# A gated mixer on one core: the last 128 columns of w2 computed turned for three chunks of four, and w3's load placed earlier in SyncE's queue

## The chip, the cores and the metric

One core of a Trainium2 chip runs the kernel. Its time is the device time of one execution in microseconds (us). Where a time is read from the profile, it is the time from the start of the profiled span.

## What is computed

Input x has 2048 rows (tokens) of D = 640 columns, bf16. The output is g·a + (1−g)·b, where g is a sigmoid of a dot product per row, a is a linear attention with 32 heads of 20 columns, and b is a mixer:

```
h  = gelu(layernorm(x) @ w1)                 # w1: 640 x 640
hs = shift(h) @ w2                           # four column groups shifted by 1, -1, 2, -2 rows; w2: 640 x 640
x1 = x + hs
b  = x1 + gelu(layernorm(x1) @ w3) @ w4      # w3: 640 x 1728, w4: 1728 x 640
a  = (phi(q) @ kv) / (phi(q) . z) @ wo       # kv and z: sums over all rows
```

The change touches `x1 = x + hs` and when w3 is loaded.

## The kernel before, in words

The rows are 16 tiles of 128 (numbered t or u), and 4 chunks of 512 (numbered c). TensorE (PE) multiplies; a matmul is at most 128x128 stationary against 512 moving columns, and a product over 640 takes five. ScalarE (ACT) applies gelu and squares, VectorE (DVE) adds into `x_tok` and normalises q, GpSimd (POOL) does the small layernorm statistics and the normalisation, and SyncE (SP) issues most DMAs, in one queue in program order. Among them are crossbar transposes ("turns", L281), which turn 128-wide blocks from SBUF to SBUF.

The stages that matter here, with short names for the steps:

- **w1(c,j)**, c = 0..3, j = 0..4 (`w1_group`, L1109): five matmuls of 512 columns, and gelu into `hsT` on ACT, shifted by rows. The fifth group (j = 4) holds parts of all four shifts, and its gelu is four ACT instructions of 32 partitions.
- **t0..t15** (`w2_tile`, L1117): for one tile, five times a 512-column matmul (L624) and a 128-column one that keeps the same stationary block (L613). DVE then adds the 640 columns of PSUM into `x_tok` and leaves the row sums (L662). The last tile of a chunk also needs rows of the next chunk: t3, t7 and t11 wait for the gelu of w1(c+1, 4).
- **sq t** (`w2_sq`, L1123): ACT squares x_tok's 640 columns and leaves the sum of squares (L680).
- **s2 c** (`ln_chunk_stats`, L859): seven small POOL instructions per chunk, after the chunk's four squares.
- **n2 u** and **T2 u** (L884, L890): POOL normalises tile u into one of three `xn` buffers; SP turns it into `xnT`. The buffer is free again when the turn has landed.
- **w3(c,j)**, j = 0..12 (`w3_group`, L1126): five matmuls of 512 columns and one gelu (`h2T`). w3(c,0) needs T2 of all four tiles of its chunk.
- **M0, M1** (`m_last`, `m_first`, L1066, L1071): the small products that make the matrix `M_sb` of the attention; ACT and DVE copy it out. **mt** (L1080): five small DMAs on SP then put rows into `M_sb`.
- **q-turn t** (L1178): SP turns the normalised q of tile t into `pqnT`.
- **a0..a15** (`a_tile`, L1229): five matmuls with `M_sb` that open the output tiles. a0 needs q-turn 0 and all five DMAs of mt.
- Then w4, the output and the end.

The order of the instructions is written neither by hand nor at run time. `_Items.run` (L336) holds each step as an item of a stream with dependencies and, at build time, always takes the item that can start first by the planner's own costs. PSUM's eight banks are given out by `bank()` (L519): the one that the planner thinks is free first. So an item that becomes later moves others, on every engine, and may make a matmul wait for another bank. Within an engine, instructions run in the planned order. x_tok is bf16; `mw` and `mtok` (L509, L510) lie in memory that the attention's `pk_tok` used earlier.

In the kernel before, w3's and w4's loads stand together on SP behind the turn of q's fourth chunk (L1377, L1378): w3 first, 2160 KB, then w4 in three DMAs, 2080 KB and twice 80 KB.

The w4 stage already computes its last 128 columns turned: `w4_turned` (L1294) multiplies with the weight block as stationary operand and 512 rows as moving columns, copies the result with ACT into `mw`, and turns it back with one DMA into `mtok`.

Of the kernel before, what the change touches and what calls it, by code (L numbers as in the profile page):

```python
# [7 lines left out]
ACTF = mybir.ActivationFunctionType  # L8
ALU = mybir.AluOpType

S = 2048
D = 640
# [3 lines left out]
NT = S // 128  # L16
NCH = S // 512
KD = D // 128
# [398 lines left out]
def _build(nc, A_x, A_wqkv, A_wo, B_w1, B_w2, B_w3, B_w4, gate_w, out, dbg=None, stop=None):  # L417
    sch = _Sched(nc)
# [41 lines left out]
    ps = nc.alloc_psum_tensor("ps", [128, 8, 512], F32)  # L460
# [10 lines left out]
    st2 = pa.alloc("st2", [128, 8, NT], F32)  # L471
# [4 lines left out]
    w2 = pa.alloc("w2", [128, KD, D], BF16)  # L476
    wo_aug = pa.alloc("wo_aug", [128, 6, D], BF16)
    x_tok = pa.alloc("x_tok", [128, NT, D], BF16)
    xnT = pa.alloc("xnT", [128, KD, S], BF16)
    hsT = pa.alloc("hsT", [128, KD, S + 4], BF16)  # L480
# [28 lines left out]
    mw = rb.alloc("mw", [128, 2, 512], BF16)  # L509
    mtok = rb.alloc("mtok", [128, 2, 4, 128], BF16)  # L510
# [8 lines left out]
    def bank():  # L519
        best = None  # L520
        for k_ in range(nbanks[0]):
            b = (bank_rr[0] + k_) % nbanks[0]
            if b in bank_pend or b in bank_hold:
                continue
            lk = sch.locks.get(b)
            tfree = 0.0 if lk is None else sch.ev_time.get((lk[1].sem, lk[1].val), 1e18)
            if best is None or tfree < best[0]:
                best = (tfree, b)
        bank_rr[0] = best[1] + 1
        bank_pend.add(best[1])  # L530
        return best[1]
# [30 lines left out]
    def nfree(ap):  # L562
        n = 1
        for d_ in ap.shape[1:]:
            n *= d_
        return n

    def in_psum(ap):
        return ap.tensor.name == ps.name

    def act(fn, reads, writes, cost=None):
        if cost is None:
            n = nfree(writes[0])
            cost = max(150.0, 100.0 + 0.833 * n + (70.0 if (reads and in_psum(reads[0])) else 0.0))
            cost += 45.0 * max(0, len(reads) - 1)
        return sch.op("act", fn, reads, writes, cost=cost)

    def dve(fn, reads, writes, cost=None):
        if cost is None:
            n = nfree(writes[0])  # L580
            cost = 65.0 + n / 0.96
        return sch.op("dve", fn, reads, writes, cost=cost)
# [7 lines left out]
    def pe(fn, reads, writes, cost=500.0, after=None):  # L590
        for w_ in writes:
            sp_, rl = sch.rects(w_)
            if sp_ == "ps":
                for (_p0, _p1, lo, hi) in rl:
                    for b in range(lo // PS_BANK, (hi - 1) // PS_BANK + 1):
                        bank_pend.discard(b)
        return sch.op("pe", fn, reads, writes, cost=cost, after=after)

    def mm_group(out_ap, pairs, reads_extra=()):
        n = len(pairs)  # L600

        def fn(e, out_ap=out_ap, pairs=pairs, n=n):
            ins = None
            for i, (l, r) in enumerate(pairs):
                ins = e.matmul(out_ap, l, r, start=(i == 0), stop=(i == n - 1))  # L605
            return ins
        reads = [a for p in pairs for a in p] + list(reads_extra)
        return pe(fn, reads, [out_ap], cost=n * (max(nfree(pairs[0][1]), 24) * 0.4167 + 2.5))
# [40 lines left out]
    def tt(engf, out_ap, a, b_, op):  # L649
        cost = None  # L650
        if engf is pool:
            cost = 1000.0 if op == ALU.pow else 200.0 + 2.3 * nfree(out_ap)
        elif not in_psum(a):
            cost = 830.0
        return engf(lambda e: e.tensor_tensor(out_ap, a, b_, op), [a, b_], [out_ap], cost=cost)  # L655

    def stt(out_ap, in0, scalar, in1, op0, op1, accum=None):
        rd = [in0, in1] + ([scalar] if not isinstance(scalar, (int, float)) else [])
        n = nfree(out_ap)
        cost = (65.0 + n / 0.96) if (in_psum(in0) or in_psum(in1)) else (160.0 + 1.04 * n)  # L660
        if accum is not None:
            return dve(lambda e: e.scalar_tensor_tensor(out_ap, in0, scalar, in1, op0, op1, accum_out=accum), rd,  # L662
                       [out_ap, accum], cost=cost + 70.0)
        return dve(lambda e: e.scalar_tensor_tensor(out_ap, in0, scalar, in1, op0, op1), rd, [out_ap], cost=cost)  # L664
# [3 lines left out]
    def activation(out_ap, in_ap, func, scale=1.0, bias=0.0, accum=None):  # L668
        rd = [in_ap] + [a for a in (scale, bias) if not isinstance(a, (int, float))]
        wr = [out_ap] + ([accum] if accum is not None else [])  # L670
        n = nfree(out_ap)
        cost = max(150.0, 100.0 + 0.833 * n + (70.0 if in_psum(in_ap) else 0.0)) + 45.0 * (len(rd) - 1)
        if accum is not None:
            cost += 91.0
        st_ = ACT_SET.get(func)
        if st_ is not None and st_ != sch.act_func:
            cost += 1290.0
            sch.act_func = st_
        if accum is not None:
            return act(lambda e: e.activation(out_ap, in_ap, func, bias=bias, scale=scale, accum_out=accum), rd, wr, cost=cost)  # L680
        return act(lambda e: e.activation(out_ap, in_ap, func, bias=bias, scale=scale), rd, wr, cost=cost)  # L681
# [105 lines left out]
    def tag_set(buf, sl, what):  # L787
        tags[(buf, sl)] = what

    def tag_chk(buf, sl, what):  # L790
        assert tags.get((buf, sl)) == what, ("stale ring slot", buf, sl, what, tags.get((buf, sl)))

    IT = _Items()
# [65 lines left out]
    def ln_chunk_stats(st, c, rs):  # L859
        cs = slice(4 * c, 4 * c + 4)  # L860
        ts(pool, st[:, 2, cs], rs, 1.0 / D, 0.0, ALU.mult, ALU.add)
        ts(pool, st[:, 3, cs], st[:, 1, cs], 1.0 / D, EPS_LN, ALU.mult, ALU.add)
        tt(pool, st[:, 4, cs], st[:, 2, cs], st[:, 2, cs], ALU.mult)
        tt(pool, st[:, 5, cs], st[:, 3, cs], st[:, 4, cs], ALU.subtract)
        tt(pool, st[:, 6, cs], st[:, 5, cs], negh[:, 0:4], ALU.pow)
        tt(pool, st[:, 7, cs], st[:, 2, cs], st[:, 6, cs], ALU.mult)
        ts(pool, st[:, 7, cs], st[:, 7, cs], -1.0, 0.0, ALU.mult, ALU.add)
# [101 lines left out]
    for i in range(3, NT + 2):  # L969
        if i < NT:  # L970
            addA(("q", i), 1.08, lambda t=i: q_tile(t))
            addA(("k", i), 1.36, lambda t=i: k_tile(t))
            if i % 4 == 3:
                addA(("qx", i // 4), 1.08, lambda c=i // 4: q_turned(c))
                IT.add("QB", ("qb", i // 4), 0.0, lambda c=i // 4: q_back(c),
                       deps=[(("qx", i // 4), 2.5), (("t1", NT - 1), 0.0) if i == NT - 1 else (("k", i + 1), 0.0)])
# [140 lines left out]
    def w2_tile(t):  # L1117
        tok = slice(2 + 128 * t, 2 + 128 * (t + 1))
        b = pair()
        mm_both((ps[:, b, 0:512], ps[:, b + 1, 0:128]), [(hsT[:, k, tok], w2[:, k, 0:512], w2[:, k, 512:D]) for k in range(KD)])  # L1120
        stt(x_tok[:, t, :], psf[:, 512 * b:512 * b + D], 1.0, x_tok[:, t, :], ALU.mult, ALU.add, accum=st2[:, 0, t:t + 1])

    def w2_sq(t):  # L1123
        activation(junk[:, 0, :], x_tok[:, t, :], ACTF.Square, accum=st2[:, 1, t:t + 1])

# [222 lines left out]
    for c in range(NCH):  # L1348
        for j in range(KD):
            deps = [(("t1", u), 0.9) for u in range(4 * c, 4 * c + 4)] if j == 0 else []  # L1350
# [7 lines left out]
    for t in range(NT):  # L1358
        c = t // 4
        deps = [(("w1", c, KD - 1), GEL)]  # L1360
        if t % 4 == 3 and c + 1 < NCH:
            deps.append((("w1", c + 1, KD - 1), GEL))
        if t == 0:
            deps.append((("g", KD - 1), 0.0))
        IT.add("W2", ("w2", t), 1.33, lambda t=t: w2_tile(t), deps)
        IT.add("SQ", ("sq", t), 0.0, lambda t=t: w2_sq(t), [(("w2", t), 1.0)])
        if t % 4 == 3:
            IT.add("S2", ("s2", c), 0.0, lambda c=c: ln_chunk_stats(st2, c, st2[:, 0, 4 * c:4 * c + 4]), [(("sq", t), 1.0)])
    for u in range(NT):
        deps = [(("s2", u // 4), 3.2 + 0.9 * (u % 4))]  # L1370
        if u >= 3:
# [2 lines left out]
            deps.append((("t1", NT - 3 + u), 0.0))  # L1374
        IT.add("N2", ("n2", u), 0.0, lambda u=u: normalize(2, u, st2), deps)
        IT.add("T2", ("t2", u), 0.0, lambda u=u: t_xn(2, u), deps=[(("n2", u), 1.1)] + ([(("mt",), 0.0)] if u == 12 else []))
    IT.add("MISC", ("w3load",), 0.0, w3_load, deps=[(("qb", NCH - 1), 0.0), (("k", NT - 1), 0.0), (("t1", NT - 1), 0.0)])  # L1377
    IT.add("MISC", ("w4load",), 0.0, w4_load, deps=[(("qb", NCH - 1), 0.0), (("kvt", 1), 0.0), (("t1", NT - 1), 0.0), (("z", NT - 1), 1.5)])  # L1378
    for c in range(NCH):
        for j in range(KFF):  # L1380
            deps = []
# [4 lines left out]
            if j == 0:  # L1386
                deps = deps0 + [(("t2", u), 0.9) for u in range(4 * c, 4 * c + 4)]
# [12 lines left out]
    for t in range(NT):  # L1400
        deps = [(("zb",), 1.0), (("q", max(t, 2)), 2.0), (("sg", 1), 0.0)]
# [13 lines left out]
    for t in range(NT):  # L1415
        g = GOF[t]
        t0, t1 = GROUPS[g]
        cl = (t1 - 1) // 4
        deps = [(("qt", t), 3.0), (("w4load",), 0.0), (("m", 1), 1.0), (("mt",), 2.5)]
# [66 lines left out]
```

## Time and profile before

| | |
|---|---|
| median of 3 runs | 259.38 us (258.87 to 259.90) |
| the profiled execution's own time | 258.86 us |
| its span | 257.6 us (1.26 us lie outside) |
| PE busy | 254.5 us, 99% of the span |
| DVE, ACT, POOL busy | 143.1, 108.5, 89.8 us |
| granted TensorE clock | 1.0 |

The span is the time from the first to the last instruction of the profiled execution. A matmul's record overlaps the next one's, so a matmul's pace is read from the distance of starts and not from its duration. The chain of work that ended last goes back from the last instruction, at each step to whatever released it. A group's line gives line number, engine, operation, out<-in tiles, shapes and count, then busy time and mean ns of one, then the idle time before them and what ended it. In the timeline, the columns are start, length, engine, line, operation, tiles and shapes; merged rows say how many instructions they hold.

### The profile page before, as it was taken

How to read it: one execution, taken by the hardware profiler on the slowest of the kernel's cores; microseconds unless marked ns; L12 is line 12 of the kernel's file. 1: busy time of each engine (PE TensorE's matmuls, PEld its weight loads, DVE VectorE, ACT ScalarE, POOL GpSimd, SP SyncE). 2: the span in 40 equal slices, each digit the busy share in tenths (PEclk: the TensorE clock that was granted, in tenths of full speed). 3: DMA queues.
4: the chain of work that ended last, by engine and by line, in shares of the span. 5: the costliest groups of instructions: out<-in, count | busy, mean ns of one | idle time of the engine just before them, and what ended most of it. 6: DMA issues, size and time to landing. Idle time of an engine off the chain costs nothing.

```text
span 257.6 us, 3610 instructions
## 1 busy us (share of the span) xinstructions
PE 254.5 (99%) x1418; PEld 110.5 (43%) x1242; DVE 143.1 (56%) x289; ACT 108.5 (42%) x222; POOL 89.8 (35%) x146
## 2 busy tenths in 40 slices
PE   8999999999999999999999999999999999999997
PEld 4333333344454333334444444444444444444444
DVE  2687888899953995489999400689300033200033
ACT  1586676651356867665854230003520100253000
POOL 5020499966762153667905200423000021300000
DMA  7878699946843699552536631022200112200012
GB/s 221 232 160 199 133 132 163 241 90 127 116 92 77 97 343 356 107 103 51 115 24 127 127 79 20 0 82 73 51 0 0 23 24 99 102 1 3 0 20 102
DMA packets 57825, 26.48 MB, mean 103 GB/s; under 512 B 49188, under 2 KB 56397, under 8 KB 57808
## 3 DMA queue, kind: packets, MB, share of 16 engines
q1 hardware_dynamic: 54976, 21.87, 38.8%
q0 software_dynamic: 1168, 3.28, 6.1%
q10 hardware_dynamic: 1664, 1.11, 1.4%
q8 instruction: 10, 0.16, 0.3%
q14 instruction: 7, 0.06, 0.1%
HBM read 12.04 MB, written 2.62 MB: 57 GB/s over the span
## 4 chain that ended last, share of the span: by engine, by line
PE 96%; DMA 2%; SPq 1%; issue 0%; DVE 0%
PE ps L605 37%; PE ps L1239 30%; PE ps L624 14%; PE ps L830 7%; PE ps L613 4%; DMA wkg<-in_A_wqkv_dram 2%; SPq L285 1%; PE ps L1285 1%; PE ps L1146 1%; PE ps L941 1%; PE ps L1028 0%; PE ps L1057 0%; DVE x_tok L664 0%
## 5 line engine op out<-in xcount | busy, mean ns | idle before, releaser
L605 PE MATMUL ps<-xnT,w 128*128 128x512 bf16 x360 | 81.3, 379 | 0.0
L664 DVE SCALAR_TENSOR_TENSOR x_tok<-ps,stg,abx 128x512 bf16<-128x512 f32 (+2 forms) x17 | 12.2, 719 | 81.9 <-PE ps L1239 81.8
L681 ACT ACTIVATE h2T<-ps 128x512 bf16<-128x512 f32 x52 | 30.6, 598 | 59.3 <-PE ps L605 59.3
L605 PEld LDWEIGHTS ps<-xnT,w 128*128 128x128 bf16 x360 | 34.5, 98 | 41.6 <-issue 2.4
L1239 PE MATMUL ps<-w,h2T 128*128 128x512 bf16 (+2 forms) x221 | 45.4, 366 | 0.0
L647 POOL TENSOR_SCALAR xn<-x_tok,st 128x640 bf16<-128x640 bf16 x32 | 34.4, 1082 | 29.2 <-DMA xnT<-xn 28.7
L647 POOL TENSOR_SCALAR abx<-x_tok,stg 128x640 f32<-128x640 bf16 (+1 forms) x16 | 15.0, 945 | 69.3 <-DVE x_tok L664 69.3
L1239 PEld LDWEIGHTS ps<-w,h2T 128*128 128x128 bf16 x221 | 21.2, 98 | 24.1
L681 ACT ACTIVATE Er<-ps 128x512 bf16<-128x512 f32 (+1 forms) x36 | 23.0, 648 | 14.6 <-PE ps L613 11.0
L680 ACT ACTIVATE junk<-x_tok 128x640 bf16<-128x640 bf16 x32 | 23.6, 738 | 3.9 <-DVE x_tok L662 3.7
L681 ACT ACTIVATE hsT<-ps 128x512 bf16<-128x512 f32 (+1 forms) x32 | 19.0, 594 | 12.5 <-PE ps L605 12.0
L624 PE MATMUL ps<-w,hsT 128*128 128x512 bf16 x80 | 23.0, 379 | 0.0
L624 PE MATMUL ps<-wkg,xT 128*128 128x512 bf16 x70 | 20.7, 379 | 0.0
L662 DVE SCALAR_TENSOR_TENSOR x_tok<-ps,x_tok 128x640 bf16<-128x640 f32 x16 | 13.1, 822 | 11.0 <-PE ps L613 10.5
L1239 PE MATMUL ps<-M_sb,pqnT 128*128 128x512 bf16 (+2 forms) x85 | 18.6, 367 | 0.0
L830 PE MATMUL ps<-pk_tok,x_tok 128*128 128x512 bf16 x80 | 17.8, 379 | 0.0
L1175 DVE TENSOR_TENSOR pq_tok<-pq_tok,dnr 128x300 bf16<-128x300 bf16 (+1 forms) x48 | 17.4, 416 | 0.5
L613 PE MATMUL ps<-wkg,xT 128*128 128x130 bf16 x80 | 17.6, 219 | 0.0
L613 PE MATMUL ps<-w,hsT 128*128 128x128 bf16 x80 | 17.5, 219 | 0.0
L647 DVE TENSOR_SCALAR Er<-Er 128x512 bf16<-128x512 bf16 (+1 forms) x36 | 12.2, 339 | 7.4 <-ACT Er L681 6.7
L605 PE MATMUL ps<-wq,xT 128*128 128x512 bf16 x65 | 16.1, 379 | 0.0
L655 DVE TENSOR_TENSOR qprod<-qprod,pk_tok 128x640 f32<-128x640 f32 x13 | 15.2, 1166 | 0.5
(90 smaller groups left out, 250.4 us busy)
## 6 DMA issues: line engine op xcount, KB each, us to landing
w<-in_B_w_dram SPq DMA_DIRECT2D x1, 2160.0 KB, 8.4
w<-in_B_w_dram SPq DMA_DIRECT2D x1, 2080.0 KB, 14.1
out_dram<-x_tok SPq DMA_DIRECT2D x3, 640.0 KB, 3.2
w<-in_B_w_dram POOLq DMA_DIRECT2D x8, 160.0 KB, 5.8
x_tok<-in_A_x_dram SPq DMA_DIRECT2D x6, 160.0 KB, 3.7
x_tok<-in_A_x_dram SPq DMA_DIRECT2D x1, 960.0 KB, 5.8
wv<-in_A_wqkv_dram POOLq DMA_DIRECT2D x1, 800.0 KB, 5.7
x_tok<-in_A_x_dram SPq DMA_DIRECT2D x1, 640.0 KB, 5.0
```

Source lines behind the costliest of these rows:

```text
L605: ins = e.matmul(out_ap, l, r, start=(i == 0), stop=(i == n - 1))
L613: return e.add_instruction(mybir.InstMatmult(name=nc.get_next_instruction_name(), engine=e.engine, ins=[e.lower_ap(r), ll], outs=[e.lower_ ...
L624: e.matmul(outs[0], l, r, start=st, stop=sp, skip_group_check=True)
L647: return engf(lambda e: e.tensor_scalar(out_ap, in_ap, s1, s2, op0, op1), rd, [out_ap], cost=cost)
L655: return engf(lambda e: e.tensor_tensor(out_ap, a, b_, op), [a, b_], [out_ap], cost=cost)
L662: return dve(lambda e: e.scalar_tensor_tensor(out_ap, in0, scalar, in1, op0, op1, accum_out=accum), rd, [out_ap, accum], cost=cost + 70.0)
L664: return dve(lambda e: e.scalar_tensor_tensor(out_ap, in0, scalar, in1, op0, op1), rd, [out_ap], cost=cost)
L680: return act(lambda e: e.activation(out_ap, in_ap, func, bias=bias, scale=scale, accum_out=accum), rd, wr, cost=cost)
L681: return act(lambda e: e.activation(out_ap, in_ap, func, bias=bias, scale=scale), rd, wr, cost=cost)
L830: ins = e.matmul(o, l, r, start=(t0 + q_ == 0), stop=(t0 + q_ == NT - 1))
L1175: dve(lambda e, o=o, i0=i0, i1=i1: e.tensor_tensor(o, i0, i1, ALU.mult), [i0, dnr[:, 1, sd, :]], [o], cost=cost)
L1239: ins = e.matmul(o, l, r, start=first and i == 0, stop=last and i == len(prs) - 1, skip_group_check=True)
```

## The change

For chunks 0 to 2, each tile's w2 product keeps the first 512 columns only (**t**, now `w2_wide`: one bank, DVE adds 512 columns). The other 128 columns are computed for a whole chunk at once, turned (**X c**, `w2_turned`): five matmuls with w2's block as stationary operand and 512 rows of `hsT` as moving columns, an ACT copy into `mw`, and one turn on SP into `mtok`. DVE then adds them tile by tile (**wt t**, `w2_tail`, 128 columns from SBUF), and only then can the squares of that tile run. The row sums come in two parts, which one more POOL instruction per chunk adds. Chunk 3 stays as it was. w3's load now stands behind the turn of q's third chunk.

```diff
+    W2T = 3
+
+    def w2_wide(t):
+        tok = slice(2 + 128 * t, 2 + 128 * (t + 1))
+        b = bank()
+        mm_group(ps[:, b, :], [(hsT[:, k, tok], w2[:, k, 0:512]) for k in range(KD)])
+        stt(x_tok[:, t, 0:512], ps[:, b, :], 1.0, x_tok[:, t, 0:512], ALU.mult, ALU.add, accum=st2[:, 0, t:t + 1])
+
+    def w2_turned(c):
+        sl = c % 2
+        b = bank()
+        mm_group(ps[:, b, :], [(w2[:, k, 512:D], hsT[:, k, 2 + 512 * c:2 + 512 * (c + 1)]) for k in range(KD)])
+        activation(mw[:, sl, :], ps[:, b, :], ACTF.Copy)
+        tag_set("mtok", sl, ("w2", c))
+        sch.dma("sp", mtok[:, sl, :, :], mw[:, sl, :], "trw%d" % sl, transpose=True)
+
+    def w2_tail(t):
+        c = t // 4
+        tag_chk("mtok", c % 2, ("w2", c))
+        stt(x_tok[:, t, 512:D], mtok[:, c % 2, t % 4, :], 1.0, x_tok[:, t, 512:D], ALU.mult, ALU.add, accum=st2[:, 3, t:t + 1])
+
+    def w2_sums(c):
+        cs = slice(4 * c, 4 * c + 4)
+        if c < W2T:
+            tt(pool, st2[:, 0, cs], st2[:, 0, cs], st2[:, 3, cs], ALU.add)
+        ln_chunk_stats(st2, c, st2[:, 0, cs])
...
-        IT.add("W2", ("w2", t), 1.33, lambda t=t: w2_tile(t), deps)
-        IT.add("SQ", ("sq", t), 0.0, lambda t=t: w2_sq(t), [(("w2", t), 1.0)])
+        turned = c < W2T
+        IT.add("W2", ("w2", t), 1.08 if turned else 1.33, lambda t=t: (w2_wide if t // 4 < W2T else w2_tile)(t), deps)
+        if turned and t % 4 == 3:
+            IT.add("W2", ("w2x", c), 1.08, lambda c=c: w2_turned(c), deps)
+            for u in range(4 * c, 4 * c + 4):
+                IT.add("WX", ("wt", u), 0.0, lambda u=u: w2_tail(u), [(("w2x", c), 5.0)])
+                IT.add("SQ", ("sq", u), 0.0, lambda u=u: w2_sq(u), [(("wt", u), 0.4)])
+        if not turned:
+            IT.add("SQ", ("sq", t), 0.0, lambda t=t: w2_sq(t), [(("w2", t), 1.0)])
         if t % 4 == 3:
-            IT.add("S2", ("s2", c), 0.0, lambda c=c: ln_chunk_stats(st2, c, st2[:, 0, 4 * c:4 * c + 4]), [(("sq", t), 1.0)])
+            IT.add("S2", ("s2", c), 0.0, lambda c=c: w2_sums(c), [(("sq", t), 1.0)])
...
-    IT.add("MISC", ("w3load",), 0.0, w3_load, deps=[(("qb", NCH - 1), 0.0), (("k", NT - 1), 0.0), (("t1", NT - 1), 0.0)])
+    IT.add("LW", ("w3load",), 0.0, w3_load, deps=[(("qb", NCH - 2), 0.0), (("k", 12), 0.0)])
```

What the planner makes of it, as the two built programs show it (the order on each engine; commas separate instructions or steps that follow each other):

```
PE before:   w1(1,0) w1(1,1) w1(1,2) t0 w1(1,3) t1 w1(1,4) w1(2,0) t2 w1(2,1) t3 w1(2,2) t4 M0 w1(2,3) t5 w1(2,4) w1(3,0)
             t6 w1(3,1) t7 w1(3,2) t8 w1(3,3) t9 w1(3,4) t10 w3(0,0) w3(0,1) t11..t15 w3(0,2)..w3(0,7) M1 w3(0,8)..w3(0,12)
             w3(1,0)..w3(1,6) a0
PE after:    w1(1,0)..w1(1,3) t0 w1(1,4) t1 t2 w1(2,0) t3 X0 w1(2,1) w1(2,2) w1(2,3) M0 t4 w1(2,4) t5 w1(3,0) t6 w1(3,1) t7
             w1(3,2) X1 w1(3,3) t8 w1(3,4) t9 t10 t11 X2 t12 t13 w3(0,0) t14 w3(0,1) t15 w3(0,2)..w3(0,9) M1 w3(0,10)..w3(0,12)
             w3(1,0)..w3(1,6) a0
ACT before:  gelu w1(3,4), sq9, w3(0,0), sq10, w3(0,1), sq11, sq12, w3(0,2), sq13, sq14, sq15, w3(0,3)..w3(0,7), M1's copies
ACT after:   gelu w1(2,4), sq0..sq3, w1(3,0)..w1(3,2), X1's copy, w1(3,3), gelu w1(3,4), sq4..sq7, X2's copy, w3(0,0), w3(0,1),
             sq8, sq9, sq10, w3(0,2), sq11..sq15, w3(0,3)..w3(0,9), M1's copies
POOL before: s2 2, n2 8, n2 9, n2 10, n2 11, s2 3, n2 12 ...
POOL after:  s2 2, n2 8, n2 9, n2 10, s2 3, n2 11, n2 12 ...
SP before:   turn of q's fourth chunk, w3, w4 (three), T2 0..11, q-turn 0, 1, 2, mt (five), q-turn 3, T2 12 ...
SP after:    (w3, behind the turn of q's third chunk) ... X0's turn, turn of q's fourth chunk, w4 (three), X1's turn, T2 0..3,
             X2's turn, T2 4..11, q-turn 0, 1, 2, mt (five), q-turn 3, 4, 5, T2 12 ...
```

M1's matmuls wait for a bank that ACT has to empty: that of w3(0,5) before, that of w3(0,8) after.

## The prediction, made before the changed kernel was run

> **What bounds the kernel now.** I read the page's busy shares first, then the chain that ended last, then PE's timeline in the w2 stage.
>
> ```profile
> span 257.6 us, 3610 instructions
> ...
> PE 254.5 (99%) x1418; PEld 110.5 (43%) x1242; DVE 143.1 (56%) x289; ACT 108.5 (42%) x222; POOL 89.8 (35%) x146
> ...
> PE 96%; DMA 2%; SPq 1%; issue 0%; DVE 0%
> ```
>
> PE is busy 99% of the span and carries 96% of the chain. So the time can fall only by less work on PE, and any new wait on PE is paid in full. The price of the matmuls, from PE's timeline (start, length):
>
> ```profile
> 112.50 0.38 PE L624 MATMUL ps<-w,hsT 128*128 128x512 bf16 x1
> 112.72 0.22 PE L613 MATMUL ps<-w,hsT 128*128 128x128 bf16 x1
> 112.77 0.38 PE L624 MATMUL ps<-w,hsT 128*128 128x512 bf16 x1
> ...
> 113.86 0.38 PE L624 MATMUL ps<-w,hsT 128*128 128x512 bf16 x1
> ...
> 125.17 13.12 PE L605 MATMUL ps<-xnT,w 128*128 128x512 bf16 x60
> 138.13 1.24 PE L1239 MATMUL ps<-M_sb,pqnT 128*128 128x512 bf16 x5
> ```
>
> By starts, a tile of w2 takes 113.86 − 112.50 = 1.36 us, and 60 matmuls of 512 take 138.13 − 125.17 = 12.96, so 0.216 each and 1.08 a group. The 128-column matmul, the rest of a pair, costs 0.272 − 0.216 = 0.056.
>
> **Part 1, PE's work.** Removed: 12 tiles x 5 x 0.056 = 3.36 us. Added: X0 to X2, 3 x 5 x 0.216 = 3.24 us. Gain 0.1 us: the columns are the same, 7680.
> [...] The rows above measure 56 and 216 in this very kernel.
>
> **Part 2, w3's load.** It now starts at about 45.2 us, after the turn at 42.91 (2.24 long), and moves 2160 KB, some 6.5 us at the 343 GB/s of slice 14. DMA share is 1.1 from 45.1 to 51.5 and 0.48 to 58.0 (windows of those stretches), so it ends near 60 and delays GT's turn and the first T1 turns by up to 2 us. Cover: T1's fourth turn, whose tile POOL finishes at 61.78, lands at about 64.5 and w1(0,0) starts at 69.7: 5 us. Cost nothing; with that cover gone, at most 2 us less what is left of it. Benefit: T2 0, at present 7.8 us in flight behind w3 and w4, lands in 2.7. But w3(0,0) waited for nothing (no idle PE at 108.98), so this frees no PE time.
>
> **Part 3, DVE and POOL.** Per chunk DVE drops 4 x about 0.13 (640 to 512 columns, 822 against 692 ns) and adds four wt of about 0.42 (the 343 ns of the same form with mtok, plus 0.08 to read the sum). Net +1.2 per chunk on an engine that idles between tiles. POOL gets three sums of 0.24. Both hidden, but for what follows.
>
> **Part 4, ACT's order, where I expect the cost.** Squares now come in fours behind a turn, and the last eight collide. The rows of ACT that price them:
>
> ```profile
> 107.83 2.44 ACT L681 ACTIVATE hsT<-ps 32x512 bf16<-32x512 f32 x4 [1.12 <-PE ps L605]
> ...
> 119.22 0.60 ACT L681 ACTIVATE h2T<-ps 128x512 bf16<-128x512 f32 x1 [0.95 <-PE ps L605]
> 119.71 0.73 ACT L680 ACTIVATE junk<-x_tok 128x640 bf16<-128x640 bf16 x1
> 120.33 0.19 ACT L680 ACTIVATION_READ_ACCUMULATOR junk<-x_tok 128x1 f32 x1
> 120.62 0.74 ACT L680 ACTIVATE junk<-x_tok 128x640 bf16<-128x640 bf16 x1
> ...
> 122.27 2.04 ACT L681 ACTIVATE h2T<-ps 128x512 bf16<-128x512 f32 x4
> ```
>
> A square in a run takes 0.92 (starts), its last 0.73; a gelu in a queue takes 0.48; the fifth w1 group 2.44; ACT starts 0.20 after PE's group ends. (The planner books 0.72 for a square.) I walk the new order with these prices, from the end of w1(1,3) on PE at 80.59 + 1.08 = 81.67:
>
> - Ten groups of 1.08, M0 (0.39), fourteen groups: t11 could start at 81.67 + 10.8 + 0.39 + 15.12 = 107.98. w1(3,4) ended at 105.82, its gelu at 105.82 + 0.20 + 2.44 = 108.46. Before, t10 and two w3 groups stood between (3.5 us); now only t9 and t10 (2.16). **First stall**: 0.5, with some 0.1 to 0.2 for restarting PE 0.65. t11 at 108.65. (t3 and t7 have 0.6 and over 1 us in hand.)
> - t11, X2, t12, t13, w3(0,0), t14, w3(0,1) take 4 x 1.08 + 3 x 1.36 = 8.4: w3(0,1) ends at 117.05. wt 8 is in time: X2's turn lands at about 115.3 and DVE is at it by 116.9.
> - ACT: w3(0,1) at 117.25, sq8 at 117.74, sq9, sq10, w3(0,2) at 120.31, sq11 at 120.8 (its sum at 121.7), sq15's sum at 125.4, w3(0,3) at 125.2, and w3(0,8) ends at 128.2. PE has finished w3(0,9) at 117.05 + 1.36 + 8 x 1.08 = 127.05 and M1 wants that bank. **Second stall**: 1.15, with the restart 1.3. M1 at 128.35; a0 could start at 128.35 + 0.67 + 10 x 1.08 = 139.8.
>
> **Part 5, the chain to a0.** Squares of chunk 2 being late (121.7; before, sq11 ended at 114.4), POOL is late, and SP behind it, since q-turns and mt stand behind T2 11:
>
> ```profile
> 114.48 0.54 POOL L647 TENSOR_SCALAR st<-st 128x4 f32<-128x4 f32 x1 [0.66 <-ACT junk L680]
> ...
> 117.90 2.61 POOL L647 TENSOR_SCALAR xn<-x_tok,st 128x640 bf16<-128x640 bf16 x3
> 121.45 1.80 POOL L647 TENSOR_SCALAR xn<-x_tok,st 128x640 bf16<-128x640 bf16 x1 [0.94 <-DMA xnT<-xn]
> 123.22 0.48 POOL L647 TENSOR_SCALAR st<-st 128x4 f32<-128x4 f32 x2
> ...
> 126.22 3.18 POOL L647 TENSOR_SCALAR xn<-x_tok,st 128x640 bf16<-128x640 bf16 x3
> ```
> ```profile
> 118.81 5.67 SPq L281 DMA_TRANSPOSE xnT<-xn  x4
> 124.52 5.32 SPq L281 DMA_TRANSPOSE pqnT<-pq_tok  x3
> 129.94 3.69 SPq L285 DMA_DIRECT2D M_sb<-Mt  x5
> ```
>
> Statistics after the last square take 3.42 here (117.90 − 114.48), 2.82 for chunk 0 (93.03 to 95.85); three normalisations 2.6 to 3.2; s2 3, which now stands ahead of n2 11, 2.8 to 3.0; n2 11 itself 0.88 to 1.80. From 121.8 that gives n2 11's end at 130.9 to 133.2; nearest the middle 132.0, against 123.25 before. From there the old run took 6.7 us to the first mt issue (three turns of about 1.3, one of them 2.68; undisturbed 5.2) and 3.07 more to the fifth (133.01). Landing isn't shown for mt; the nearest row is an output of 32 KB, 1.5 us, and the next 1.8; I take 1.7. So mt lands at 132.0 + 6.2 + 3.07 + 1.7 = 143.0 (140.6 to 145.0 with all ends), where before it landed near 134.7, 3.4 us ahead of a0. **Third stall**: 143.0 − 139.8 = 3.2. a0 starts near 142.9, 4.8 later than at 138.13.
>
> Behind a0 nothing catches up or falls back further: T2 15 follows five turns after mt and lands at about 152, and its reader comes ten groups and a half-group behind a0, at 154; then PE runs as before.
>
> **Sum.** 258.86 + 4.8 = 263.7 us (part 1's 0.1 is in the walk). The profiled run lies 0.5 below the median of the three shown, so 263.7 to 264.2; I say **263.9**. With the ends of part 5, a0 is 2.5 to 6.9 late: 261.3 to 265.8 on its own time, 266.3 on the median's.
>
> **Rivals.**
> - *Only ACT's two stalls.* If POOL and SP run at their fast ends and mt lands by 139.8, a0 is 1.7 late: 260.5. For it: qt's 2.68 and n2 11's 1.80 are single outliers. Against it: even all fast ends together give 140.6.
> - *Not slower.* With w3 gone from SP, T2 0 is 5 us quicker, POOL (6.14 idle for xnT at 104.73) gets chunks 0 and 1 out of the way, and squares 8 to 10 find ACT free. Place: sq11. Price: only the first stall is left, 259.4. It decides if sq11 ends by about 115, so that mt lands by 138. Against it: sq8 stands behind the gelu of w3(0,1), which PE cannot finish before 116.4 even without any stall.
> - *Slower than that.* PE's idle at a0 is long enough to slow its clock. The opening matmuls (L903) averaged 626 ns against 379; if the 3 us after the stall ran at half pace, 1.5 more: 265.4, and with the late end of part 5 267.3. The granted clock is 1.0 in every window I read, so no row shows this inside the span. [...]
> - *The load costs.* The early w3 delays the T1 turns past 69.7: up to 1 us more. Against it: 5 us of cover.
>
> **Chances.** Forecast (261.3 to 266) 0.73; only ACT's stalls 0.09; not slower 0.06; slower by the clock or the load, above 266, 0.09; faster by something not seen 0.03. The range reaches from the rival with ACT's stalls alone to the late end on the median's base: 260.5 to 266.4. Half a per cent, 1.3 us, is about what a measurement here can tell from no change: faster 0.03, same 0.08, slower 0.89.
>
> **What would show it.** PE idle ahead of t11 (0.6), M1 (1.3) and a0 (3.2), released by ACT, ACT and a DMA; sq11 near 120.8; n2 11 near 131; mt's first issue near 138. If a0 starts without a wait, part 5 is wrong; if M1 does, part 4. If PE's pace in X differs from 1.08, part 1.

## The result, and the profile after

| | before | after |
|---|---|---|
| median of 6 runs each | 259.15 us (258.87 to 259.90) | 266.56 us (264.89 to 267.92) |
| the profiled execution's own time, its span | 258.86, 257.6 us | 267.86, 266.6 us |
| PE busy | 254.5 us, 99% | 256.4 us, 96% |
| DVE, ACT, POOL busy | 143.1, 108.5, 89.8 us | 144.5, 110.8, 90.4 us |
| mean granted clock, run by run | 1.0 | 1.0 (264.89 us), 0.994 (266.21, 266.40, 266.72), 0.987 (267.86, 267.92) |
| a0 starts | 138.13 us | 144.43 us |

The changed kernel is slower: 1.029 times the time before, 95% interval 1.0263 to 1.0316. The forecast was 263.9, its range 260.5 to 266.4. The runs after fall into three levels 1.5 us apart, one for each granted clock. That is the first thing to notice. (Of the kernels further below, one run of the four with chunk 3's squares late took 545.36 us at full clock; the median given there counts it, the ratio leaves it out.)

The page of the kernel after: the granted clock in 40 slices, and the chain that ended last by engine.

```profile
PEclk9999999999999999999997799999999999999999
...
PE 85%; ACT 4%; DVE 3%; DMA 3%; issue 2%; POOL 2%; ACTq 0%; POOLq 0%
```

PE is down from 99% to 96%. The clock row has two slices below full speed, the 22nd and 23rd (140.0 to 153.3 us); before there was none. The chain was 96% PE before; now ACT, DVE, POOL, DMA and PE's own waiting ("issue") carry 14%. PE's timeline shows where (start, length, what; in brackets the idle time before it and what ended it):

```profile
109.11 1.04 PE L605 MATMUL ps<-w,hsT 128*128 128x512 bf16 x4 [0.37 <-ACT hsT L681]
...
114.69 1.24 PE L605 MATMUL ps<-xnT,w 128*128 128x512 bf16 x5 [0.53 <-DMA xnT<-xn]
...
129.23 0.74 PE L1057 MATMUL ps<-wo_aug,Lt 60*64 60x512 bf16 x16 [0.87 <-ACT h2T L681]
...
144.84 1.91 PE L1266 MATMUL ps<-M_sb,pqnT 128*128 128x512 bf16 x4 [3.97 <-issue]
146.54 2.34 PE L605 MATMUL ps<-xnT,w 128*128 128x512 bf16 x5
148.68 1.86 PE L1266 MATMUL ps<-M_sb,pqnT 128*128 128x512 bf16 x5
```
```profile
144.43 0.14 PEld L1266 LDWEIGHTS ps<-M_sb,pqnT 128*128 128x128 bf16 x2 [4.06 <-issue]
```

Read the brackets from top to bottom: t11 waits for the gelu of w1(3,4); w3(0,0), which had not waited before, for a turn of xn; M1 for ACT; and a0, L1266 now, for longest. Its 3.97 us is too long: a0 has five matmuls, the trace holds four (x4) and five weight loads (PEld), the first at 144.43. So the record of its first matmul is missing; a0 starts near 144.43, and PE is idle for 3.56 us ahead of it. The loss is 0.1 to 0.2 us more than the idle time (0.37, 0.53, 0.87 and 3.56): by starts, 0.54, 0.70, 1.0 and 3.7 (M1 ends at 129.90, where the weight loads of the next group begin, and ten groups of 1.08 end at 140.70). Then three groups of 1.08 take 2.11, 2.14 and 1.69 us by starts (the next begins at 150.37 and takes 1.08, the old pace): 2.7 us more than at full speed. Here are a0's wait and the slower groups as stretches of 3.38 us (PE busy time, number of matmuls, granted clock, DMA share, GB/s):

```profile
139.70:143.08 3.38, 1.17 (x6) 1.00 0.06 13
143.08:146.46 3.38, 1.62 (x4) 0.50 0.49 97
146.46:149.84 3.38, 3.38 (x9) 0.50 0.54 108
```

The clock was halved from 143.08 to about 149.9, 6.8 us or twice 3.4, and nowhere else in the span: (1 − 0.987) x 266.6 = 3.5 us is what half of 6.8 gives. 0.994 is one such stretch. So one stretch of 3.4 us costs about 1.5 us, since PE needs most of it, and the three levels of the runs are none, one and two.

Behind a0's wait stand POOL and SP, whose timelines answer to the lines of before in the prediction:

```profile
122.84 0.25 POOL L647 TENSOR_SCALAR st<-st 128x4 f32<-128x4 f32 x1 [1.70 <-ACT junk L680]
...
128.77 0.48 POOL L647 TENSOR_SCALAR st<-st 128x4 f32<-128x4 f32 x2
...
131.95 3.15 POOL L647 TENSOR_SCALAR xn<-x_tok,st 128x640 bf16<-128x640 bf16 x3
```
```profile
134.11 4.81 SPq L281 DMA_TRANSPOSE pqnT<-pq_tok  x3
139.01 4.16 SPq L285 DMA_DIRECT2D M_sb<-Mt  x5
```

POOL waits for sq11 until 122.84 (114.48 before), does s2 2 and n2 8 to 10, then s2 3, and n2 11 only at 131.95 (121.45 before). On SP, mt is issued from 139.01 (129.94 before); the last of the five is issued at 142.55, and a0 starts 1.9 us later.

Sum at a0, in the profiled executions: t11 0.5, w3(0,0) 0.7, M1 1.0, a0 3.7, less part 1's 0.1, and 0.5 by which w1(1,3) already ended later (82.17 for 81.67) = 6.3, which is 144.43 − 138.13. (The expectations below took the recorded 144.84 for a0's start and say 3.9 for its wait.) With the clock's 2.7 it is 9.0, the difference of the spans. The 0.5 was there before the load was issued (43.41 for 42.91 at the turn of q's third chunk) and before any changed product ran. I don't count it to the change: the kernel with the load alone starts a0 0.49 late in its profiled execution (138.62), and the last experiment 0.64 late (138.77), both without a wait and with the median of before.

### The profile page after: what moved, and what is told of

Same layout as the page of the kernel before. It is cut to its first block, busy times and chain, and to the rows that moved or that the text cites. A ratio compares the mean times of both kernels' runs of the same rounds, so it can differ in the third digit from the quotient of the medians.

```text
span 266.6 us, 3578 instructions
## 1 busy us (share of the span) xinstructions
PE 256.4 (96%) x1348; PEld 113.1 (42%) x1257; DVE 144.5 (54%) x313; ACT 110.8 (42%) x225; POOL 90.4 (34%) x149
## 4 chain that ended last, share of the span: by engine, by line
PE 85%; ACT 4%; DVE 3%; DMA 3%; issue 2%; POOL 2%; ACTq 0%; POOLq 0%
PE ps L605 33%; PE ps L1266 30%; PE ps L624 7%; PE ps L830 6%; DMA xnT<-xn 3%; PE ps L613 2%; PE ps L941 2%; ACT junk L680 2%; ACT h2T L681 1%; PE ps L903 1%; DVE x_tok L662 1%; PE ps L1312 1%; POOL xn L647 1%; ACT hsT L681 1%; PE ps L1173 1%
## 5 line engine op out<-in xcount | busy, mean ns | idle before, releaser
L664 DVE SCALAR_TENSOR_TENSOR x_tok<-ps,stg,abx 128x512 bf16<-128x512 f32 (+2 forms) x17 | 12.2, 718 | 85.9 <-PE ps L1266 85.8
L605 PEld LDWEIGHTS ps<-xnT,w 128*128 128x128 bf16 x360 | 35.1, 98 | 43.7 <-issue 2.9
L1266 PE MATMUL ps<-w,h2T 128*128 128x512 bf16 (+2 forms) x216 | 45.2, 366 | 0.3
L647 POOL TENSOR_SCALAR abx<-x_tok,stg 128x640 f32<-128x640 bf16 (+1 forms) x16 | 14.2, 894 | 70.2 <-DVE x_tok L664 70.2
L1266 PEld LDWEIGHTS ps<-w,h2T 128*128 128x128 bf16 x221 | 21.2, 98 | 24.1
L1266 PE MATMUL ps<-M_sb,pqnT 128*128 128x512 bf16 (+2 forms) x81 | 19.4, 387 | 4.3 <-issue 4.3
L662 DVE SCALAR_TENSOR_TENSOR x_tok<-ps,x_tok 128x512 bf16<-128x512 f32 (+1 forms) x16 | 11.5, 720 | 11.0 <-PE ps L605 9.0
L681 ACT ACTIVATE mw<-ps 128x512 bf16<-128x512 f32 x7 | 4.2, 597 | 30.5 <-PE ps L1266 28.9
L1202 DVE TENSOR_TENSOR pq_tok<-pq_tok,dnr 128x300 bf16<-128x300 bf16 (+1 forms) x48 | 16.5, 398 | 0.6
L647 DVE TENSOR_SCALAR Er<-Er 128x512 bf16<-128x512 bf16 (+1 forms) x36 | 12.2, 339 | 7.0 <-ACT Er L681 6.3
L1266 PEld LDWEIGHTS ps<-M_sb,pqnT 128*128 128x128 bf16 x85 | 8.3, 102 | 14.7 <-issue 6.9
## 6 DMA issues: line engine op xcount, KB each, us to landing
w<-in_B_w_dram SPq DMA_DIRECT2D x1, 2160.0 KB, 12.2
```

The lines of the kernel that those rows point to most:

```text
L647: return engf(lambda e: e.tensor_scalar(out_ap, in_ap, s1, s2, op0, op1), rd, [out_ap], cost=cost)
L1202: dve(lambda e, o=o, i0=i0, i1=i1: e.tensor_tensor(o, i0, i1, ALU.mult), [i0, dnr[:, 1, sd, :]], [o], cost=cost)
L1266: ins = e.matmul(o, l, r, start=first and i == 0, stop=last and i == len(prs) - 1, skip_group_check=True)
```

## The experiments

The theory: PE's work is the same; all the loss is waits that the new order makes. The one that counts is a0's, at the end of a chain over ACT, POOL and SP; the clock fell in it, at 143.08 us. Rivals: the early load costs; the turned columns cost something on whatever engine; SP's transfers hold a0, whoever comes before. The times in the second column are medians, the starts of a0 and the waits are read from one profiled execution of each; "before" was measured beside each set at 258.94 to 259.39.

| run | median us | ratio to before, 95% | a0 starts (profiled) | PE's waits left |
|---|---|---|---|---|
| load only | 259.36 | 0.9992 to 1.0011 | 138.62 | none |
| turned columns only | 266.05 | 1.0207 to 1.0334 | 145.30 | t11, w3(0,0), M1, a0 |
| filler ahead of a0 | 265.29 | 1.0209 to 1.0240 | 144.69 | the same, a0's filled |
| mt first | 262.15 | 1.0091 to 1.0140 | 141.27 | t11, w3(0,0), M1, a0 0.56 |
| s2 3 behind n2 11 | 262.86 | 1.0138 to 1.0169 | 142.36 | t11, w3(0,0), M1, a0 1.25 |
| chunk 3's squares late | 264.73 | 1.0197 to 1.0238 | 142.27 | t11, w3(0,0), a0 2.29 |
| three moves | 261.60 | 1.0090 to 1.0127 | 140.91 | w3(0,0) 1.75, a0 0.21 |
| two chunks turned | 265.39 | 1.0236 to 1.0288 | 144.59 | t11 1.17, t14 1.55, a0 3.03 |
| two chunks, s2 3 moved | 262.95 | 1.0136 to 1.0169 | 141.92 | t11 1.17, t14 1.55 |
| both moves | 259.96 | 1.0026 to 1.0050 | 139.65 | t11 0.37, w3(0,0) 0.48 |
| no wait at t11 either | 259.22 | 0.9992 to 1.0011 | 138.77 | none |

### The load alone

The kernel before, with w3's load where the change puts it:

```diff
-    IT.add("MISC", ("w3load",), 0.0, w3_load, deps=[(("qb", NCH - 1), 0.0), (("k", NT - 1), 0.0), (("t1", NT - 1), 0.0)])
+    IT.add("LW", ("w3load",), 0.0, w3_load, deps=[(("qb", NCH - 2), 0.0), (("k", 12), 0.0)])
```

> The kernel before, with w3's load alone moved behind the turn of q's third chunk; every other order is as before. The theory (the early load is hidden) expects the time of before, 259.1 within 0.6, with a0 near 138. A rival, that the early load costs, expects 0.5 to 1 more, and that it shows as a later w1(0,0), because the changed kernel's w1 and w2 stages ran 0.5 us later than before from the start.

Measured 259.36, ratio 0.9992 to 1.0011, clock 1.0, no wait on PE. The load neither costs nor gains. In the changed kernel it landed 12.2 us after its issue, at 56.9, far ahead of its first reader.

### The turned columns alone

The changed kernel with the line above turned round (the load at its old place).

> The changed kernel with w3's load at its old place, behind X0's turn and the turn of q's fourth chunk and ahead of w4's; all orders but SP's are the changed kernel's. The theory (the turned columns cost, the early load does not) expects a time no better than the changed kernel's 266.6, and probably 267 to 270: X1's turn and T2 0 to 2 then queue behind 4.4 MB of loads, so wt 4 to 7 and w3(0,0) come later. The rival, that the early load is what costs, expects 259 to 262.

Measured 266.05. The two runs at clock 1.0 gave 265.06 and 265.08, where the changed kernel's one such run gave 264.89; the others, 267.01 and 268.83, lost one and two stretches of clock (0.994 and 0.987). So the whole loss comes with the turned columns, and the late load makes it no worse. That it would be worse was a miss. w3 has landed at 102.2, before X1's turn and T2 0 are issued (104.84 and 106.97), since the squares of chunk 0 are late as well; w4 lands only at 108.4 to 109.1, and X1's turn takes 4.6 us instead of 2.4, but w3(0,0) waits no longer than in the changed kernel (0.40 us idle for 0.53).

### A filler in a0's wait

The changed kernel with 16 matmuls of a constant ahead of a0, into the bank that a0 then overwrites:

```diff
+            if t == 0:
+                def fill(e, b=b):
+                    one = nc.const_aps.tensor(1.0, [128, 512], BF16)
+                    ...
+                    for _ in range(16):
+                        ins = e.matmul(ps[:, b, 0:512], one[:, 0:128], one[:, 0:512], start=True, stop=True)
```

> The changed kernel, with 16 matmuls of constants (16 x 0.216 = 3.5 us) ahead of a0, into the bank that a0 overwrites with its first matmul; all orders are the changed kernel's. The theory (the idle time before a0 lets the clock drop, and that costs some 2.3 us after it) expects a0 to start at the same place, the granted clock 1.0 in every run, and 264.3 to 265.2 with less spread than the changed kernel's 264.9 to 267.9. The rival, that the clock's drop has another cause or costs nothing, expects 266 to 268 again; if the filler itself delays a0, 266 and up with the clock at 1.0.

PE's timeline of this kernel:

```profile
140.99 3.66 PE L1264 MATMUL ps<-const-bfloat16-1.0 128*128 128x512 bf16 x16
144.69 1.24 PE L1274 MATMUL ps<-M_sb,pqnT 128*128 128x512 bf16 x5
```

a0 starts no earlier, but the next group follows after 1.07 us (at 145.76). The granted clock was 1.0 in all four runs, and they lie within 0.22 us of each other (265.20 to 265.42; the median of 265.29 is 0.1 above what was expected). The loss of clock is caused by the idle time, and is worth 1.3 us in the median and 2.5 in the slowest runs.

### mt first

```diff
-    IT.add("MT", ("mt",), 0.0, m_tail, deps=[(("m", 1), 1.5), (("qt", 2), 0.0)])
+    IT.add("MT", ("mt",), 0.0, m_tail, deps=[(("m", 1), 1.5)])
```

> The changed kernel with mt no longer tied to q-turn 2, so that SP issues its five small DMAs right behind T2 11 and ahead of q-turn 0; PE's, ACT's and DVE's orders are the changed kernel's. The theory (a0 waits for mt, which stands too late in SP's queue) expects mt to land near 140, q-turn 0 near 141, a wait of 0.2 to 0.6 ahead of a0 in place of 3.9, the clock at 1.0, and 261.0 to 262.0. The rival, that a0 waits for what POOL normalises or for ACT and not for mt, expects 265 to 267.

SP and PE of this kernel:

```profile
134.01 4.11 SPq L285 DMA_DIRECT2D M_sb<-Mt  x5
```
```profile
141.27 1.25 PE L1266 MATMUL ps<-M_sb,pqnT 128*128 128x512 bf16 x5 [0.56 <-DMA pqnT<-pq_tok]
```

mt goes out 5 us earlier, behind T2 11 and ahead of the q-turns, which follow from 138.56. a0 now waits for q-turn 0, and for 0.56 us only; the clock stays at 1.0; 262.15, which is 0.15 above what was expected. The three waits before a0 are as they were. So taking away most of a0's wait, and the loss of clock with it, is worth 4.4 us of the 7.4.

### s2 3 behind n2 11

On POOL only; the order on PE and ACT stays.

```diff
-            IT.add("S2", ("s2", c), 0.0, lambda c=c: w2_sums(c), [(("sq", t), 1.0)])
+            IT.add("S2", ("s2", c), 0.0, lambda c=c: w2_sums(c), [(("sq", t), 1.0)] + ([(("n2", 11), 0.0)] if c == 3 else []))
```

> The changed kernel, but chunk 3's statistics on POOL (s2 3) stand behind n2 11 instead of ahead of it; PE's and ACT's orders stay. Theory (a0 is held by the chain squares of chunk 2, s2 2, n2 8 to 11, T2 11, three q-turns, mt): n2 11 began at 131.95 behind s2 3; now it follows n2 10, which ends at about 128.8, but it needs the buffer of n2 8, whose turn lands 2.7 to 3.6 us after its issue at about 127, so n2 11 begins at 129.7 to 130.6. That is 1.4 to 2.3 earlier, and so is mt: a0's wait falls from 3.9 to 1.6 to 2.6, too short for a lower clock (granted clock 1.0). From 265.3 (the run with filler, clock 1.0): 263.0 to 263.9 us. Rival (the queue of SP and the latency of its transfers hold a0, whatever POOL's order): 264.9 to 266.5, a0's wait over 3.4.

n2 11 on POOL in this kernel:

```profile
130.03 0.88 POOL L647 TENSOR_SCALAR xn<-x_tok,st 128x640 bf16<-128x640 bf16 x1 [1.00 <-DMA xnT<-xn]
```

n2 11 starts at 130.03 instead of 131.95, held by its buffer as expected, and a0 at 142.36 instead of 144.43; the wait is 1.25, a little less than expected, and 262.86 a little below the expected 263.0. The granted clock was 1.0 in all four runs; that a wait of up to 2.6 us is too short for a lower clock was my assumption, and with the squares late, below, 2.29 us lowered it. The rival with SP alone (264.9 or more) is out: POOL's order sets when SP can begin.

### Chunk 3's squares late

```diff
-            IT.add("SQ", ("sq", t), 0.0, lambda t=t: w2_sq(t), [(("w2", t), 1.0)])
+            IT.add("SQ", ("sq", t), 0.0, lambda t=t: w2_sq(t), [(("w2", t), 1.0), (("w3", 0, 8), 0.0)])
```

> The changed kernel, but the four squares of chunk 3 may run only behind w3(0,8): ACT does the gelus of w3(0,3) to w3(0,10) first, M1 stands behind w3(0,6), and s2 3 falls behind n2 11 by itself. Theory (the waits do not add: a0 starts when mt has landed, whatever was lost before): M1's wait of 1.0 is gone and a0 can be reached 1.0 earlier, but mt lands as in the run with s2 3 moved, so a0's wait is 1.0 longer than there and the time the same within 0.5: 262.8 to 264.0 us, clock 1.0 if the wait stays under 3.4. Rival (each wait costs by itself): 1.0 less than the run with s2 3 moved, 261.9 to 262.9.

a0 on PE's timeline, and two stretches of 3.38 us around it (the clock is at 1.00 again from 145.5):

```profile
142.27 2.29 PE L1266 MATMUL ps<-M_sb,pqnT 128*128 128x512 bf16 x5 [2.29 <-issue]
```
```profile
138.70:142.08 3.38, 1.28 (x6) 1.00 0.06 15
142.08:145.46 3.38, 3.19 (x8) 0.50 0.66 132
```

M1 (125.11) no longer waits, and a0 starts at 142.27, within 0.1 of the run before it, where M1 did wait. The waits do not add up: a0 starts when mt has landed, and what is saved ahead of it only makes its own wait longer (2.29 for 1.25). And the longer wait cost the clock one stretch, in each of the three runs of about 264.6 us (0.994), so the kernel with one wait less is 1.9 us slower, 264.73. The mechanism was as expected; the time was missed, because I took 3.4 us of idle as the limit. No run shows that limit: 2.29 us was enough here.

### Three moves

The squares late, mt first, and t8 tied to w1(3,4):

```diff
+        if t == 8:
+            deps.append((("w1", 3, KD - 1), 0.0))
```

> The changed kernel with all products turned as there, and three orders altered: t8 to t11 stand behind w1(3,4) (so t11 has five groups between it and the gelu that it needs, and w3(0,0) comes behind t15), chunk 3's squares behind w3(0,8), and mt not tied to q-turn 2 (it stands ahead of T2 11). Theory (the turned columns themselves cost PE nothing, all the loss is in waits that the order makes): no wait at t11, w3(0,0), M1; mt is issued from about 129.2, q-turn 0 from about 133.7 and lands by 137.3, before a0 at about 138.5: no wait there. Left is the 0.5 by which w1(1,3) is late: 259.2 to 260.2 us. Rival (the additional turns, adds and squares fill an engine whatever the order): 261 to 263.

SP and PE:

```profile
107.64 1.19 SPq L281 DMA_TRANSPOSE mtok<-mw  x1
108.88 4.74 SPq L281 DMA_TRANSPOSE xnT<-xn  x3
...
114.97 17.65 SPq L281 DMA_TRANSPOSE xnT<-xn  x8
```
```profile
118.19 8.79 PE L605 MATMUL ps<-xnT,w 128*128 128x512 bf16 x40 [1.75 <-DVE x_tok L662]
```

261.60, missed by 1.4, and within the rival's bounds; what tells the two apart is where PE waits. t11 and M1 do not wait, but w3(0,0) does, 1.75 us. The profile names DVE, whose add of t15 was long done; T2 3 was issued at 114.97 and landed 3.0 us later, at 117.9, which fits the start at 118.19. The move had put X1's turn behind w1(3,4) and so ahead of T2 0 to T2 2. X1's turn took 5.1 us (issued 107.64; its reader on DVE started at 112.81) where the changed kernel had 2.4, T2 0 landed only at 113.57, 4.7 us after its issue, and n2 3, which needs T2 0's buffer, started at 113.66: T2 3 was late. What else moved then (queue, kind, packets, MB, share; then the turn, with us to landing), from 107.6 to 110:

```profile
q8 instruction: 1, 0.02, 3.4%
...
mtok<-mw SPq DMA_TRANSPOSE x1, 5.1
```

A transfer of kind "instruction" passed beside the two slow turns (the last section has more on this). Had T2 0 landed in 2.6 us, n2 3 could have started 2.1 us earlier, more than the whole wait; so part of this miss may be where that transfer fell, and no run separates it from the order. Either way the repaired wait had come back through another queue.

### Two chunks turned, and the same with s2 3 moved

```diff
-    W2T = 3
+    W2T = 2
```

> The changed kernel with two chunks turned (0 and 1) instead of three; chunk 2 is computed as before the change. Theory (what costs is that chunk 2's rows are whole only after X2's turn, so that sq8 to sq11 are late): sq11 runs near 116 instead of 121.9 and a0 does not wait; M1 waits 0 to 0.5. But only t10 stands between w1(3,4) and t11, so t11 waits 1.3 to 1.5 for the gelu, and w3(0,0) 0 to 0.5: 260.5 to 261.8 us, clock 1.0. Rival (each turned chunk costs its share, two thirds of 7.4): 263.6 to 264.6.

265.39: a clear miss, a0 waits 3.03 us. POOL:

```profile
121.07 3.17 POOL L647 TENSOR_SCALAR xn<-x_tok,st 128x640 bf16<-128x640 bf16 x3
...
125.83 1.25 POOL L647 TENSOR_SCALAR st<-st 128x4 f32<-128x4 f32 x2
...
129.26 3.15 POOL L647 TENSOR_SCALAR xn<-x_tok,st 128x640 bf16<-128x640 bf16 x3
```

These are n2 5 to n2 7, the start of s2 3 and n2 9 to n2 11 (n2 8 stands between, at 124.67). sq11 ran at 117.68, 4.3 us earlier than in the changed kernel, and it did not help. Chunk 1's rows were late by X1's turn and its squares, so its normalisations run until 126, then s2 3, and only then n2 9 to n2 11, at 129.26 to 132.4. That corrects the theory: not the squares of chunk 2 as such, but the place of n2 11 in POOL's queue holds a0, and each late chunk pushes it back. Besides, t11's add waited for sq10 in this program (DVE idle for 5.0 us until ACT's square ended), so banks came free late and t14 waited 1.55, which I had not seen. The corrected theory was put to the test by moving s2 3 here as well:

> Two chunks turned, as in the run before it, and chunk 3's statistics on POOL moved behind n2 11; PE's and ACT's orders as there. In that run sq11 ran 4.3 us earlier than in the changed kernel, and a0 still waited 3.0: on POOL, n2 5 to n2 8 (late because chunk 1's squares stand behind X1's turn) and s2 3 (3.4 us) stood ahead of n2 9 to n2 11, so n2 11 began at about 131.4. Corrected theory (what holds a0 is the place of n2 11 in POOL's queue): n2 11 ends 2.3 to 3.2 us earlier, a0 waits 0 to 0.8, 262.3 to 263.2 us, clock 1.0; left are the waits at t11 (1.2) and at t14 for a bank (1.6). Rival (SP's queue and the waits before a0 set it): 264.7 to 265.6.

262.95, within the expected bounds: a0 follows the last w3 group with 0.3 us lost by starts, and the waits at t11 and t14 stay as they were.

### Both moves, and t11's wait taken away too

Three chunks turned, mt first and the squares late; then the same with t8 behind w1(3,4), and X1 kept where it was by one more dependency:

```diff
+            if (c, j) == (3, 3):
+                deps.append((("w2x", 1), 0.0))
```

> The changed kernel with three chunks turned, mt not tied to q-turn 2, and chunk 3's squares behind w3(0,8). Each alone left one wait in force: with mt first M1 still waited for ACT, with the squares late a0 still waited for mt. Theory: together neither is left; mt goes out behind T2 10 (from about 130.4), q-turn 0 from about 135.4 and lands at 138.1 to 139.0, a0 can be reached at 139.9: no wait. Left are the 0.5 of w1(1,3), t11's 0.5 and w3(0,0)'s 0.6: 260.5 to 261.1 us, granted clock 1.0. Rival (one of the queues was covered by these waits and now shows): above 261.5.

259.96 (ratio 1.0026 to 1.0050), 0.5 below what was expected; neither M1 nor a0 waits.

> As the run with both moves, and also t8 to t11 behind w1(3,4), with X1 kept ahead of w1(3,3): four groups stand between w1(3,4) and t11, more than the 2.64 that its gelu takes, and w3(0,0) comes behind t15. Theory (only waits cost, the turned columns do not): t11's wait is gone; X2's turn stands ahead of T2 3, which lands at about 117.2, so w3(0,0), reached at 116.2, waits up to 1.0; a0 0 to 0.3: 259.5 to 260.9 us. If w3(0,0) does not wait, it is the first version within 0.5 of the kernel before. Rival (turning loses its share elsewhere): above 261.5.

PE's timeline of the last kernel has no bracket left from w1(3,4) to a0; w3(0,0) and a0 read:

```profile
116.42 8.79 PE L605 MATMUL ps<-xnT,w 128*128 128x512 bf16 x40
...
138.77 1.24 PE L1266 MATMUL ps<-M_sb,pqnT 128*128 128x512 bf16 x5
```

259.22 (258.70 to 259.68), ratio 0.9992 to 1.0011: the time of the kernel before, with all three chunks turned. T2 3 had landed (116.17) when w3(0,0) came up at 116.42, the better of the two cases expected, and the time is 0.3 below the bounds. This settles it: the turned columns cost PE nothing and gain it nothing that can be measured; the 7.4 us were order, and four changed dependencies take them back. No version was faster than the kernel before.

## Why the prediction was right or wrong

- **Part 1, right.** X1 takes 1.08 us by starts (102.10 to 103.18), and the last experiment has the time of before with the same columns turned. The price of a matmul in this kernel is 0.056 us for 128 columns and 0.216 for 512.
- **Part 2, right.** The load alone: 259.36. The benefit to T2 0 was smaller than I put it: it landed in 3.6 us, not 2.7. The load itself took 12.2 us and landed at 56.9, before the 60 that I had.
- **Part 3, too large.** DVE's busy time grew by 1.4 us in all, where I had 1.2 for each of three chunks. No bracket above names DVE, though its adds now stand ahead of the squares and DVE carries 3% of the chain that ended last.
- **Part 4, right in mechanism and close in size.** t11 0.54 for 0.65, M1 1.0 for 1.3, both released by ACT. Missed: w3(0,0) waits 0.70 for T2 3. I had walked ACT for chunks 2 and 3, but not POOL and SP for chunk 0, whose n2 0 started at 105.22 (95.85 before), because chunk 0's squares stand behind X0's turn and the gelu of w1(2,4).
- **Part 5, right in mechanism, too small.** mt landed near 144.4 where I had 143.0: sq11 ended 1.0 later (122.75 for 121.7, of which 0.7 is w3(0,0) and 0.5 the late start), n2 11 0.8 later (132.8 for 132.0), five mt issues took 0.5 more, and landing 1.9 instead of 1.7. The slow turn that I called a single outlier came again on the way (T2 11 landed in 4.6 us, q-turn 0 took 2.16 to issue). The third stall was 3.7 for 3.2. The one run with the full clock, 264.89, is 5.7 above before; I had 4.8. That any new wait on PE is paid in full, as I began, does not hold ahead of a0: with the squares late M1's wait is gone and a0 starts where it did, because it waits for mt.
- **The step that failed is the clock.** The rival "slower than that" had the right mechanism and the right price for one stretch (1.5 us), but together with the load I gave it 0.09 and left it outside the range, because the granted clock was 1.0 in every window before. The trace before had no wait to trip it. In the sum the clock cost nothing; in five of six runs a stall of 3.7 us lost one or two stretches, 1.3 to 3.0 us each time. With a stall forecast at 3.2 and ends to 5, that term belonged in the sum with a good share. It puts the median 1.7 us above the run with the full clock, and past the range's end by 0.16.
- **The rival "not slower" named a wrong condition.** It was to decide at sq11, by 115 us. In the run with both moves n2 11 ended at 130.4 and a0 still did not wait, because mt no longer stood behind it. The condition was a place in SP's queue, not a time on ACT.

## What to carry to other kernels

When a producer is made later by a detour, walk each chunk through every in-order queue behind it (here ACT, POOL, SP), and not only the last one; the end is set by one item's place in those queues, so repairing a wait ahead of it may bring nothing. Price an expected stall on TensorE with the clock as well: here 2.29 us of idle cost one stretch of 3.4 us at half speed, about 1.5 us, in three of three runs, and 3.56 us one or two in five of six. And before giving up a change whose work is neutral, see whether an added dependency or two restores the order.

## What was not expected of the hardware

- The clock fell in stretches of 3.4 us (142.08 to 145.49 with the squares late, and twice that in the changed kernel, 143.09 to 149.91), and the length of the gap alone does not tell whether it does: 2.29 us of idle tripped it in three of three runs of about 264.6 us (squares late), 3.03 us in only one of four (two chunks turned: 266.71 us at 0.994, the rest 265.31 to 265.48 at 1.0), 3.56 us in five of six (the changed kernel). What else decides it is not shown by an experiment.
- PE was not idle throughout just before the fall: it was busy for 1.17 of 3.38 us in the changed kernel, for 1.28 of 3.38 (38%) with the squares late, and for 0.78 of 3.37 with the turned columns alone. With two chunks turned, the clock of the profiled execution stayed at full speed through the gap (start and end, length, PE busy, clock, DMA share, GB/s):

```profile
141.60:144.60 3.00, 0.01 (x1) 1.00 0.07 15
```

- After a first stretch at half clock with PE busy for 2.0 of 3.4 us (the changed kernel, a0 from 144.43 on) a second followed, and so it did with 2.3 (turned columns alone); after one with 3.2 (squares late) it did not.
- A turn on SP sometimes took far longer than 2.4 us (128x512) or 2.7 (128x640), and a row of turns is not the reason: T2 4 to T2 7 of the changed kernel, issued one behind the other from 116.46, landed in 2.6 to 2.7 us each. What the slow ones have beside them is a transfer of kind "instruction" (16 KB on q8 or 8 KB on q14 in the traces). Of the 308 turns issued on SP between 100 and 150 us in the 13 profiled executions, 221 had none in flight beside them, and 220 of these landed within 2.8 us; of the 87 that had one, 47 took over 2.9 us, up to 5.1. That the transfer is the cause is not shown by an experiment.
